# A fused gated recurrence and MLP: the first product in seven block products over two of its three feature tiles, and no latency inside an engine in the plan

## The chip, the cores and the metric

The kernel runs on one core of a Trainium2 chip. The core has a matrix engine (TensorE, PE in the profile; its weight loads are PEld), a vector engine (DVE), an activation engine (ACT), GpSimd (POOL) and a queue engine (SP), each of which works through its own instruction list in order. They wait for each other through semaphores. The metric is the device time in microseconds (us) of a whole execution. A second record of the same kernel is the profile of one execution, whose span goes from its first to its last instruction.

## The reference, cut to what matters

A gated linear recurrence over 768 positions for 4 x 8 heads of 48 features gives 3072 tokens of 384 features. They go through a two-layer block with the activation h - tanh(h).

```python
for t in range(S):                      # per batch and head
    state = alpha[t][:, None] * state + k[t][:, None] * v[t][None, :]
    y[t] = q[t] @ state
x = y.transpose(0, 2, 1, 3).reshape(3072, 384)
h = x @ w_in                            # 384 -> 2048
g = h - tanh(h)
return g @ w_out                        # 2048 -> 384
```

All is float32. The kernel takes h - tanh(h) as a polynomial in h, and checks on the chip that the arguments are small enough for it.

## The kernel before, in words

**Tiles and loops.** The 3072 tokens are cut into 12 units (NU) of 256 tokens (TU), that is two token tiles of 128. For each unit `gla(u)` does the recurrence in a chunked form and leaves the unit's tokens transposed in `xT[u]`: 128 features by 256 tokens in each of three feature tiles (KT = 3). A fourth feature tile is working space; `moves` copies 16-row pieces from it into the first three by DMA. Then `moe(u)` goes over 8 steps (FS), each with two tiles of 128 of the 2048 hidden features. There are two buffers of `xT`.

**One step.** `first` (line 1078) computes h for two hidden tiles a and the unit's 256 tokens: for each a three products, one per feature tile j, of a 128 x 128 weight block and 256 token columns (line 1083). h fills one of two PSUM banks (`ps_h`). On ACT, `square` (line 1092) makes u from h squared and `quad` (line 1096) makes z from u. On DVE, `cube` (line 1100) multiplies h and u into w, and `shrunk` (line 1104) makes g from z and w. After two steps `large` (line 1110, ACT) looks for arguments that are too big. For units from the third on (`PLAIN` = 2) the second product is itself a block product with seven terms: `sums` (lines 1116 to 1118, DVE) makes five combinations e of blocks of g, and `second` (line 1149) does seven products of 192 columns onto four PSUM accumulators o, with weight combinations b that `combine 0` to `combine 4` have made from w_out once. Units 0 and 1 use line 1128 instead. After eight steps `store` takes the accumulators out.

**Buffers.** u, z and w have two buffers (u holds two steps in each), g and e have three. A bank of h is free when `cube` has read it.

**The order.** It isn't the program's order of loops. A `Planner` gets every piece of work as a task with an engine, a duration in us, a rank and the names of the tasks that it waits for. It simulates the engines: the start of a task is after the ends of those it waits for, plus a latency (0.3 us unless the task says otherwise, whatever the two engines are). It does eight rounds of list scheduling with priorities from the latest starts, keeps the round that ends earliest, and issues the instructions in that order. Two tasks that follow in a chain of the same kind without a named dependence have latency 0 on the same engine. On the chip semaphores alone decide when an instruction runs; the plan fixes only each engine's order. Idle PE time at the beginning is filled with products of an identity matrix (line 1211).

**Work beside the steps.** The recurrence of a later unit (on DVE: 32 x 32 transposes at line 641, scans at 713 and 732, scalings at 737, and smaller sums; on ACT: copies at 635, 918 and 999), and `look`, which reloads weights and checks their size on ACT (lines 104 and 105).

Of the kernel before, what the change touches and what calls it, by code (L numbers as in the profile page):

```python
# [9 lines left out]
FP32 = mybir.dt.float32  # L10
# [7 lines left out]
P = 128  # L18
HP = 64
CU = 2  # L20
# [301 lines left out]
class Planner:  # L322
# [13 lines left out]
    def add(self, name, engine, us, rank, after, do, lat=0.3):  # L336
        kind = name.rsplit(" ", 1)[0]
        self.tasks.append((name, engine, us, rank, [a for a in after if a], do, lat, self.last.get(kind)))
        self.last[kind] = name
# [47 lines left out]
    def order(self):  # L387
        names = {t[0]: i for i, t in enumerate(self.tasks)}
        assert len(names) == len(self.tasks)
        before, after = ([[] for _ in self.tasks] for _ in range(2))  # L390
        for i, t in enumerate(self.tasks):
            edges = {names[a]: self.tasks[names[a]][6] for a in t[4]}
            if t[7]:
                edges.setdefault(names[t[7]], 0.0 if self.tasks[names[t[7]]][1] == t[1] else 0.25)
            for j, lat in edges.items():
                before[i].append((j, lat))
                after[j].append((i, lat))
# [17 lines left out]
        for x in plan:  # L415
            name, e, length = self.tasks[x[3]][:3]
            if e == engine and until:
# [3 lines left out]
                free = x[0] + length  # L421
# [5 lines left out]
def fast(tc, q, k, v, alpha, moe_w_in, moe_w_out, out, w_in, w_out, ident, ok, pad_rows):  # L427
# [11 lines left out]
    NH = d_model // 2  # L439
    PLAIN = 2  # L440
    V, A, T, GP = nc.vector, nc.scalar, nc.tensor, nc.gpsimd

    out_r = out.rearrange("(t p) n -> t p n", p=P)

    with ExitStack() as ctx:
# [159 lines left out]
        def gla(u, rank):  # L605
# [166 lines left out]
            def chunk(c):  # L772
# [7 lines left out]
                def go_c(name, engine, us, k, after, do, **kw):  # L780
                    add(f"{name} {me}", engine, us, rank + 6 * c + k,
                        [a if a[-1] in "0123456789" else f"{a} {me}" for a in after if a], do, **kw)
# [200 lines left out]
                if not last:  # L983
                    go_c("state", "DVE", 0.26, 10, ["mid", n > 0 and not past_last and f"y {past}"], state)
                go_c("y", "PE", 1.29, 9, ["masked", "mid", not last and "state", n > 0 and "decay",
                                         u == 1 and c and f"x {past}", u == 1 and c and f"rest {past}"], halves_products)
                go_c("x", "ACT", 0.5, 10, ["y"], features)
                go_c("rest", "DVE", 0.87 if u >= PLAIN else 1.02, 10.5, ["x"], rest)

# [60 lines left out]


        looked = {}

# [13 lines left out]
        def moe(u, rank, gait):  # L1067
            m = {}
            plain = u < PLAIN

            def step(s):
# [15 lines left out]

                def square():
                    if s % 2 == 0:
                        m["us", s // 2] = two.tile([P, 2, 2 * TU], FP32, name="u")  # L1090
                    m["u", s] = m["us", s // 2][:, s % 2]
                    A.activation(m["u", s], m["h", s], AF.Square, scale=W_SCALE ** -1.5)  # L1092

# [4 lines left out]
                def cube():  # L1098
                    m["w", s] = two.tile([P, 2 * TU], FP32, name="w")
                    V.tensor_mul(m["w", s], m["h", s], m["u", s])  # L1100
# [18 lines left out]

                def second():  # L1120
                    g = m["g", s]
                    if plain:
# [7 lines left out]
                        return  # L1130
                    if s == 0:
                        m["o"] = [ps_o.tile([P, 2, NH], FP32, name=f"o{n}") for n in range(2 * CU)]
# [10 lines left out]
                    if u == NU - 1 and s == FS - 2:  # L1143
                        now, m["rest"] = now[:4], now[4:]
                    elif u == NU - 1 and s == FS - 1:
                        now = now[:4] + m["rest"][:2] + now[4:6] + m["rest"][2:] + now[6:]

                    for s_, n, i, g_, w_ in now:
                        T.matmul(o[n][:, i], lhsT=g_, rhs=w_, start=(s_ == 0 and (n, i) in ((0, 0), (1, 0), (2, 1), (3, 0))),  # L1149
                                 stop=(s_ == FS - 1), skip_group_check=True)  # L1150

                add(f"first {me}", "PE", 2.59, r,
                    [f"in{s}" if plain else None, f"cube {older[2]}" if older[2] else f"masked 0.{CU - 1}"]
                    + [f"x {u}.{c}" if u == 0 else f"moves {u}" for c in range(CU if u == 0 else 1)], first)

                add(f"square {me}", "ACT", 0.5, r + 0.9,
                    [f"first {me}"] + ([f"large {older[3]}", f"cube {older[3]}", f"quad {older[3]}"]
                                       if s % 2 == 0 and older[3] else []), square)
                add(f"cube {me}", "DVE", 0.6, r + 0.9, [f"square {me}", older[2] and f"shrunk {older[2]}"], cube)
# [5 lines left out]
                if not plain:  # L1165
                    add(f"sums {me}", "DVE", 0.85, r + 1.1, [f"shrunk {me}"], sums)
                add(f"second {me}", "PE", 2.58 if plain else 1.3 if me == f"{NU - 1}:{FS - 2}" else 3.28 if me == f"{NU - 1}:{FS - 1}" else 2.28, r + 5,
                    [f"out{s}" if plain else "combine 4", f"sums {me}" if not plain else f"shrunk {me}"]
                    + ([f"store {n}" for n in range(max(0, u - 2 if u <= PLAIN else u - 1), u)] if s == 0 and u >= PLAIN else [])
                    + ([f"state {PLAIN - 1}.{c}" for c in range(CU) if (PLAIN - 1) % UPB * CU + c < NCH - 1]  # L1170
                       + [f"rest {PLAIN - 1}.{CU - 1}"] if u == PLAIN - 1 and s == 0 else [])
                    + ([f"second {u}:{s - 1}"] if s else []), second)

# [151 lines left out]
```

## Time and profile before

| | us |
|---|---|
| median of three runs | 576.95 (576.02 to 577.92) |
| the profiled execution, span | 574.2 |
| PE busy | 564.0 |
| DVE busy | 450.9 |
| ACT busy | 323.2 |
| one step's first product (line 1083, 12 records), in the chain | 2.59 |
| one unit in the steady stretch | 44.80 |

The profiled execution has only its span, from first to last instruction; no total of that execution is recorded. The 2.75 us between the span and the median of the runs are what lies around the instructions, and the difference between executions. Busy time is the union of an engine's intervals. Ends of matrix instructions are modelled, so the start of the next one is the better mark. A float32 product appears as two records. A group's line gives the source line, engine, operation, output and inputs with shapes, the count, busy time and mean duration in ns, and the idle time ahead of it with what ended it.

### The profile page before, as it was taken

How to read it: one execution, taken by the hardware profiler on the slowest of the kernel's cores; microseconds unless marked ns; L12 is line 12 of the kernel's file. 1: busy time of each engine (PE TensorE's matmuls, PEld its weight loads, DVE VectorE, ACT ScalarE, POOL GpSimd, SP SyncE). 2: the span in 40 equal slices, each digit the busy share in tenths (PEclk: the TensorE clock that was granted, in tenths of full speed). 3: DMA queues.
4: the chain of work that ended last, by engine and by line, in shares of the span. 5: the costliest groups of instructions: out<-in, count | busy, mean ns of one | idle time of the engine just before them, and what ended most of it. 6: DMA issues, size and time to landing. Idle time of an engine off the chain costs nothing.

```text
span 574.2 us, 13772 instructions
## 1 busy us (share of the span) xinstructions
PE 564.0 (98%) x5595; PEld 498.0 (87%) x5595; DVE 450.9 (79%) x886; ACT 323.2 (56%) x559; POOL 4.8 (1%) x22
## 2 busy tenths in 40 slices
PE   8999999999999999999999999999999999999995
PEld 8877677778999989998998999899898999899995
DVE  6988879999999996896895895896797745544643
ACT  3689996747687675676584374364353433333530
POOL 3000000000000000000000000000000000000000
PEclk9999999999999999999999999999999999999999
DMA  8889792336674852562630320310200000000001
GB/s 179 200 223 252 254 169 63 93 77 137 114 143 122 171 116 93 117 144 85 169 114 7 82 60 2 84 50 14 58 8 1 30 7 3 29 8 0 29 2 34
DMA packets 60713, 50.84 MB, mean 89 GB/s; under 512 B 35776, under 2 KB 50400, under 8 KB 60640
## 3 DMA queue, kind: packets, MB, share of 16 engines
q1 hardware_dynamic: 57728, 48.88, 34.8%
q10 hardware_dynamic: 2912, 0.98, 0.8%
q8 instruction: 46, 0.75, 0.6%
q14 instruction: 27, 0.22, 0.1%
HBM read 44.04 MB, written 4.72 MB: 85 GB/s over the span
## 4 chain that ended last, share of the span: by engine, by line
PE 95%; DMA 2%; SPq 1%; ACT 1%; DVE 0%; issue 0%; POOL 0%; DVEq 0%; ACTq 0%; POOLq 0%
PE h L1083 42%; PE o L1149 33%; PE o L1128 7%; PE sc L808 2%; PE sc L881 2%; PE sc L814 2%; PE sc L891 2%; DMA raw<-in_moe_w_in_dram 2%; PE sc L994 1%; PE spin L1211 1%; SPq L43 1%; PE turned L665 1%; PE scores L798 0%; SPq L597 0%; PE sc L665 0%
## 5 line engine op out<-in xcount | busy, mean ns | idle before, releaser
L1083 PE MATMUL h<-xT,w_in 128*128 128x256 f32 x1152 | 265.5, 380 | 1.2 <-DVE w_in L90 1.1
L1083 PEld LDWEIGHTS h<-xT,w_in 128*128 128x128 f32 x1152 | 215.2, 190 | 29.4 <-DVE w_in L90 2.7
L1092 ACT ACTIVATE u<-h 128x512 f32<-128x512 f32 x96 | 56.9, 592 | 175.3 <-PE h L1083 174.8
L1100 DVE TENSOR_TENSOR w<-h,u 128x512 f32<-128x512 f32 x96 | 66.0, 689 | 79.0 <-ACT u L1092 78.7
L1149 PE MATMUL o<-b,e 128*128 128x192 f32 x480 | 90.9, 326 | 0.0
L1149 PE MATMUL o<-w_out,e 128*128 128x192 f32 x320 | 81.4, 337 | 0.0
L1149 PEld LDWEIGHTS o<-b,e 128*128 128x128 f32 x480 | 80.2, 190 | 0.0
L1104 DVE SCALAR_TENSOR_TENSOR g<-z,w 128x512 f32<-128x512 f32 x96 | 65.7, 685 | 3.1 <-ACT z L1096 0.2
L1149 PE MATMUL o<-b,g 128*128 128x192 f32 x320 | 65.1, 326 | 0.0
L1096 ACT ACTIVATE z<-u 128x512 f32<-128x512 f32 x96 | 60.4, 629 | 2.6
L1149 PEld LDWEIGHTS o<-w_out,e 128*128 128x128 f32 x320 | 55.7, 190 | 4.4
L1149 PEld LDWEIGHTS o<-b,g 128*128 128x128 f32 x320 | 54.2, 190 | 0.0
L1110 ACT ACTIVATE big<-u 128x1024 f32<-128x1024 f32 x48 | 50.4, 1050 | 0.0
L1128 PE MATMUL o<-w_out,g 128*128 128x384 f32 x128 | 44.0, 488 | 0.0
L1128 PEld LDWEIGHTS o<-w_out,g 128*128 128x128 f32 x128 | 24.1, 190 | 13.7
L1116 DVE TENSOR_TENSOR e<-g 128x256 f32<-128x256 f32 x80 | 33.6, 420 | 1.8
L1117 DVE TENSOR_TENSOR e<-g 128x256 f32<-128x256 f32 x80 | 33.5, 419 | 0.0
L641 DVE STREAM_TRANSPOSE aT<-ar 128x256 f32<-128x256 f32 x44 | 28.4, 646 | 2.8 <-ACT ar L635 1.7
L732 DVE TENSOR_TENSOR_SCAN W<-aT,before 128x1032 f32<-128x1032 f32 (+1 forms) x13 | 27.8, 2135 | 0.0
L713 DVE TENSOR_TENSOR_SCAN U<-aT,after 128x1032 f32<-128x1032 f32 (+1 forms) x13 | 27.6, 2128 | 0.1
L1118 DVE TENSOR_TENSOR e<-g 128x128 f32<-128x128 f32 x80 | 22.9, 287 | 0.0
L86 ACT ACTIVATE more<-raw 128x768 int16<-128x768 uint32 x16 | 17.2, 1074 | 7.1 <-DMA raw<-in_moe_w_out_dram 2.8
(138 smaller groups left out, 559.9 us busy)
## 6 DMA issues: line engine op xcount, KB each, us to landing
raw<-in_moe_w_out_dram SPq DMA_DIRECT2D x16, 768.0 KB, 5.2
raw<-in_moe_w_in_dram SPq DMA_DIRECT2D x80, 96.0 KB, 4.4
raw<-in_moe_w_in_dram SPq DMA_DIRECT2D x16, 288.0 KB, 4.7
vt<-in_v_dram SPq DMA_DIRECT2D x23, 192.0 KB, 4.4
ar<-in_alpha_dram SPq DMA_DIRECT2D x44, 96.0 KB, 2.7
kr<-in_k_dram SPq DMA_DIRECT2D x40, 96.0 KB, 2.3
qr<-in_q_dram SPq DMA_DIRECT2D x40, 96.0 KB, 2.3
out_dram<-cross SPq DMA_DIRECT2D x19, 96.0 KB, 1.7
```

What stands on the lines that cost most here:

```text
L641: V.transpose(to, raws[what][:, g, :, 0:32])
L732: V.tensor_tensor_scan(out=m["W"][:, ns].rearrange("p n t -> p (n t)"), data0=aT[:, a:z], data1=before[:, a:z], initial=0.0, op0=ALU.mult, ...
L1083: T.matmul(h[:, a, :], lhsT=w_in[:, j, f * P:(f + 1) * P], rhs=xT[u][:, j, :], start=(j == 0), stop=(j == KT - 1))
L1092: A.activation(m["u", s], m["h", s], AF.Square, scale=W_SCALE ** -1.5)
L1096: A.activation(m["z", s], m["u", s], AF.Square, bias=QB, scale=QA * W_SCALE)
L1100: V.tensor_mul(m["w", s], m["h", s], m["u", s])
L1104: V.scalar_tensor_tensor(out=g.rearrange("p a c t -> p (a c t)"), in0=m["z", s], scalar=QK, in1=m["w", s], op0=ALU.add, op1=ALU.mult)
L1110: A.activation(big, m["us", s // 2].rearrange("p s t -> p (s t)"), AF.Relu, bias=-U_FAST, scale=W_SCALE, accum_out=over[:, n:n + 1])
L1116: V.tensor_add(e[:, 0:2, :], g[:, 0], g[:, 1])
L1117: V.tensor_sub(e[:, 2:4, :], g[:, :, 1, :], g[:, :, 0, :])
L1128: T.matmul(m["o"][c], lhsT=g[:, a, c, :], rhs=w_out[:, f, :], start=(f == 0), stop=(f == FT - 1))
L1149: T.matmul(o[n][:, i], lhsT=g_, rhs=w_, start=(s_ == 0 and (n, i) in ((0, 0), (1, 0), (2, 1), (3, 0))), stop=(s_ == FS - 1), skip_group_ch ...
```

## The change

**The first product.** For units from the fourth on (`SEVEN` = 3), two feature tiles and two hidden tiles against two token tiles form a 2 x 2 block product, which is done with seven products of 128 columns instead of eight (as four of 256 columns). The third feature tile is done as before, two products of 256 columns. The seven need combinations of weight blocks and of token blocks:

- `weigh 0` to `weigh 4` (DVE, once) make four combinations of w_in over all steps, three of them in a part of w_out that is no longer read, one in place of a block of w_in.
- `mix u` (DVE, per unit) makes four combinations of token blocks, in the fourth feature tile of `xT`, in a new tile, and in place of one block.

A step's product becomes a chain: two products, a copy on ACT of both results into u; a third product added onto one of them, a copy; a fourth added onto the same, a copy; three more, each onto one quarter; the third feature tile onto all four quarters. `join` on DVE adds the bank and the kept copies into w, and `square` and `cube` read w instead of the bank. The bank is free after `join`. `second` is issued in four tasks of 2, 2, 1 and 2 products, except in the last two steps.

**The plan.** The latency between two tasks of one engine, SP left out, is 0 instead of 0.3 us. The task `x` gets a named dependence on the last first product of two units before.

```diff
-            edges = {names[a]: self.tasks[names[a]][6] for a in t[4]}
+            edges = {names[a]: 0.0 if self.tasks[names[a]][1] == t[1] != "SP" else self.tasks[names[a]][6] for a in t[4]}
...
+    SEVEN = 3
...
-                go_c("x", "ACT", 0.5, 10, ["y"], features)
+                go_c("x", "ACT", 0.5, 10, ["y", u > 1 and f"first {u - 2}:{FS - 1}"], features)
...
+        wi = w_in.rearrange("p k (s a n) -> p k s a n", a=2, n=P)
+        free = w_out.rearrange("p (s a) n -> p s (a n)", a=2)[:, :, NH:3 * NH].rearrange("p s (i n) -> p s i n", n=P)
+        left = {1: wi[:, 0, :, 0], 2: wi[:, 1, :, 0], 3: free[:, :, 2], 4: wi[:, 1, :, 1], 5: free[:, :, 0], 6: free[:, :, 1], 7: wi[:, 0, :, 1]}
+        def weigh(n):
+            if n == 0:
+                V.tensor_add(left[5], wi[:, 0, :, 1], left[4])
+            elif n == 1:
+                V.tensor_sub(left[6], left[5], left[1])
+            elif n == 2:
+                V.tensor_sub(left[3], left[2], left[6])
+            else:
+                at = slice((n - 3) * FS // 2, (n - 2) * FS // 2)
+                V.tensor_sub(left[7][:, at], left[1][:, at], left[7][:, at])
+        for n in range(5):
+            add(f"weigh {n}", "DVE", 1.2 if n < 3 else 0.7, 2 * FS * (SEVEN - 1) + (n if n < 3 else 8 * (n - 2)),
+                ["combine 4", f"second {PLAIN - 1}:{FS - 1}"] + [n > 2 and f"first {SEVEN - 1}:{(n - 2) * FS // 2 - 1}"], lambda n=n: weigh(n))
+        def mix(u):
+            x, more = xT[u], combo_pool[0].tile([P, P], FP32, name="more_x", bufs=2)
+            (b11, b12), (b21, b22) = ([x[:, k, h * P:(h + 1) * P] for h in range(2)] for k in range(2))
+            t1, t2 = (x[:, KT, h * P:(h + 1) * P] for h in range(2))
+            right[u] = {1: b11, 2: b21, 3: b22, 4: more, 5: t1, 6: t2, 7: b12}
+            V.tensor_sub(t1, b12, b11)
+            V.tensor_sub(t2, b22, t1)
+            V.tensor_sub(more, b21, t2)
+            V.tensor_sub(b12, b22, b12)
...
+                def product(n, to, start=False):
+                    T.matmul(m["h", s][:, to], lhsT=left[n][:, s], rhs=right[u][n], start=start, stop=True, skip_group_check=True)
+                def seven_a():
+                    m["h", s] = ps_h.tile([P, 4, P], FP32, name="h")
+                    product(1, 3, True)
+                    product(5, 1)
+                def keep(n):
+                    if n == 0:
+                        take_u()
+                        m["kept", s] = m["u", s].rearrange("p (i t) -> p i t", t=P)
+                        A.copy(m["kept", s][:, 0::3], m["h", s][:, 3::-2])
+                    else:
+                        A.copy(m["kept", s][:, n], m["h", s][:, 3])
+                def seven_d():
+                    for n, to in ((2, 0), (3, 1), (4, 2)):
+                        product(n, to)
+                def seven_e():
+                    for a in range(2):
+                        T.matmul(m["h", s][:, 2 * a:2 * a + 2].rearrange("p i t -> p (i t)"), lhsT=wi[:, KT - 1, s, a], rhs=xT[u][:, KT - 1, :],
+                                 start=False, stop=True, skip_group_check=True)
+                def join():
+                    m["w", s] = two.tile([P, 2 * TU], FP32, name="w")
+                    V.tensor_add(m["w", s], m["h", s].rearrange("p i t -> p (i t)"), m["u", s])
+                    m["h", s] = m["w", s]
...
+                if seven:
+                    add(f"first_a {me}", "PE", 0.45, r, [bank, f"mix {u}", "weigh 0"], seven_a)
+                    add(f"keep_a {me}", "ACT", 0.38, r + 0.1, [f"first_a {me}"] + old_u, lambda: keep(0))
+                    add(f"first_b {me}", "PE", 0.224, r + 0.2, [f"keep_a {me}", "weigh 1"], lambda: product(6, 3))
+                    add(f"keep_b {me}", "ACT", 0.26, r + 0.3, [f"first_b {me}"], lambda: keep(1))
+                    add(f"first_c {me}", "PE", 0.224, r + 0.4, [f"keep_b {me}", f"weigh {3 + 2 * s // FS}"], lambda: product(7, 3))
+                    add(f"keep_c {me}", "ACT", 0.26, r + 0.5, [f"first_c {me}"], lambda: keep(2))
+                    add(f"first_d {me}", "PE", 0.67, r + 0.6, [f"keep_c {me}", "weigh 2"], seven_d)
+                    add(f"first {me}", "PE", 0.86, r + 0.65, [f"first_d {me}"], seven_e)
+                    add(f"join {me}", "DVE", 0.65, r + 0.7, [f"first {me}", older[2] and f"shrunk {older[2]}"], join)
...
+                parts = [7] if not seven or (u == NU - 1 and s >= FS - 2) else [2, 4, 5, 7]
```

## The prediction

> **What bounds the kernel now.** I read the page first (busy times, the 40 slices, the chain that ended last, the costliest groups), then stretches of one unit each, then single groups.
>
> ```profile
> PE 564.0 (98%) x5595; PEld 498.0 (87%) x5595; DVE 450.9 (79%) x886; ACT 323.2 (56%) x559; POOL 4.8 (1%) x22
> PE   8999999999999999999999999999999999999995
> DVE  6988879999999996896895895896797745544643
> ACT  3689996747687675676584374364353433333530
> PE 95%; DMA 2%; SPq 1%; ACT 1%; DVE 0%; issue 0%; POOL 0%; DVEq 0%; ACTq 0%; POOLq 0%
> L1083 PE MATMUL h<-xT,w_in 128*128 128x256 f32 x1152 | 265.5, 380 | 1.2 <-DVE w_in L90 1.1
> L1149 PE MATMUL o<-b,e 128*128 128x192 f32 x480 | 90.9, 326 | 0.0
> ```
>
> 95% of the chain is PE, and the two groups show almost no idle time before them: TensorE is the bound, and nothing it waits for matters. Each float32 product has two records (1152 for 576 products). The next view gives busy time by engine for the opening units of the changed stretch, two middle ones and the last full ones.
>
> ```profile
> core 0: us, PE busy (x) PEld busy (x) DVE busy (x) ACT busy (x) POOL busy (x), PEclk, DMA share, GB/s
> 137.00:167.50 30.50, 30.50 (x320) 28.19 (x310) 30.24 (x63) 21.90 (x42) 0.00 (x0) 1.00 0.63 121
> 167.50:212.30 44.80, 44.80 (x474) 40.94 (x474) 43.68 (x86) 33.41 (x62) 0.00 (x0) 1.00 0.67 144
> 257.10:301.90 44.80, 44.80 (x472) 40.94 (x473) 37.06 (x76) 31.23 (x58) 0.00 (x0) 1.00 0.43 122
> 346.70:391.50 44.80, 44.80 (x458) 40.94 (x457) 36.47 (x74) 20.95 (x37) 0.00 (x0) 1.00 0.18 48
> 436.30:481.10 44.80, 44.80 (x474) 40.94 (x473) 25.61 (x61) 16.23 (x28) 0.00 (x0) 1.00 0.04 13
> 481.10:525.90 44.80, 44.80 (x396) 41.06 (x395) 23.79 (x54) 15.33 (x27) 0.00 (x0) 1.00 0.04 12
> ```
>
> Unit 3, the first to change, starts its first products at 167.5, and every unit takes 44.80 us, all PE. DVE has 7 to 8 us to spare per unit in the middle, 1 us in unit 3, and 19 us and more at the end.
>
> The chain in order of time gives the price of a step:
>
> ```profile
> 251.12 2.61 PE h L1083 x12
> 330.24 2.59 PE h L1083 x12
> 558.42 4.55 PE o L1149 x28
> ```
>
> A first product is 2.59 us, 0.4325 per product of 256 columns; a second one 2.28 (7 x 0.326). 8 x 4.87 = 38.96 of the 44.80 are these; 5.84 is the recurrence of the unit ahead.
>
> **What the skill says.** The Trainium skill, TensorE: Matmul & The Clock Gate, LDWEIGHTS: a load takes its columns over 1.2, so 107 ns for 128. A 128-column product has two loads beside two passes, so loads could bound it. The trace has such a product, the idle filler:
>
> ```profile
> 10.54 1.38 PE L1211 MATMUL spin<-ident 128*128 128x128 f32 x10
> L923 ACT COPY xT<-y 128x256 f32<-128x256 f32 x1 | 0.4, 372 | 0.6 <-PE y L863 0.6
> L923 ACT COPY xT<-y 128x128 f32<-128x128 f32 x1 | 0.3, 272 | 0.0
> L1100 DVE TENSOR_TENSOR w<-h,u 128x512 f32<-128x512 f32 x96 | 66.0, 689 | 79.0 <-ACT u L1092 78.7
> ```
>
> The first gap is 0.213 (cold start) and the last record lasts 0.275, so the eight gaps between are (1.38 - 0.213 - 0.275) / 8 = 0.112 us, and a product of two costs 0.2235, load and pass in step; the page's price agrees. The same page, table at the head: ACT and DVE are strict first-in first-out, PE can only pull loads ahead. That decides how a late wait spreads. ScalarE: Activation LUTs, What ACT_TABLE_LOAD costs: 186 ns + 0.833 ns an element; 293 for 128, the trace has 272. VectorE: DVE Perf Modes, the perf-mode tier table: float32 tensor_tensor has one rate, SBUF or PSUM; the trace agrees (689 with a PSUM input, 685 at line 1104 without).
>
> **Removed and added on PE.** Per step, six products of 256 (2.595) become seven of 128 (7 x 0.2235 = 1.5645) and two of 256 (0.865): 2.4295. The saving is 0.1655; 9 units x 8 steps = 72 steps give **11.9 us**, the most the change can bring. The second product is cut into parts of 2, 2, 1 and 2 products, with no further instruction: free, as PE changes between the two kinds now at no visible gap.
>
> **The chain it adds.** Products 1 and 5, a copy on ACT, product 6 onto the same columns, a copy, product 7, a copy, three products, then the third tile. Each copy must end before PE goes on. In the timeline line 1083's last pass starts at 404.91 and takes 0.216, and ACT starts at 405.33, 0.20 us after it; from a copy's end to PE's start it shows 0.05 (38.19 to 38.24, line 1002 to line 814). So the three loops are 0.20+0.37+0.05 = 0.62, and twice 0.20+0.27+0.05 = 0.52: 1.66 us a step. Bare, that is 120 us over 72 steps. The cover: four parts of a second product (2.28), the other h bank's chain, and 5.84 / 8 = 0.73 of recurrence per step. That is more than enough if it is ready. The plan prices the loops 0.98 and twice 0.86, so each has some 0.35 of slack against the trace. Two banks: a bank comes back after about 5 us of chain plus join, and two steps last 10.6, so the banks do not bind.
>
> Queued behind a late wait on PE is everything, second products and the recurrence's too; behind a copy on ACT, the squares and so the cubes. The trace of before shows no PE wait of this sort in the steady stretch, so I bound it: 0 if the plan's slack holds; and above, one keep in five late by 0.3 us, 216 x 0.2 x 0.3 = 13 us, all of the gain. I take one in ten by 0.2, that is 4.3 us: the slack speaks for few, ACT's long pieces (1.05 + 0.19 for line 1110, 1.8 for a look) for some.
>
> **ACT** gains 0.372 + 2 x 0.272 = 0.92 a step, 7.3 a unit. With 33.4 that is 40.7 of 43.5 in unit 3; with 20.95 it is 28. The square reads SBUF instead of PSUM: 629 against 592, 0.3 a unit.
>
> **DVE** gains the join, 0.69 (5.5 a unit), and mix, four dependent 128-column operations, some 0.29 each: 1.15. With 36.5 that is 43.1 against a new PE unit of 44.80 - 1.32 = 43.48; in unit 3, with 43.68, it is 50.3, besides weigh (three at 1.22 as at line 737, two at 0.69: 5 us, partly before 167.5). That is over. What hides it is work ahead: in the timeline the recurrence of unit 4 (line 903) ends on DVE at 192.6, for products that start at 212.3, 20 us early. Units 3 to 8 can spend that, then the recurrence ends and DVE is at 75%. So DVE's sum does not bind, but its queue is full, so joins and sums come late at times. I put this at 0.2 to the same 4.3 us, no further term; none and 8 us as its ends.
>
> **The plan without in-engine latency.** It adds no instruction and only reorders, in units 0 to 2 too. The engines run as soon as they can, and dependent DVE operations cost 0.72 from start to start (line 1104 at 405.24, line 1116 at 405.96) where the plan now says 0.60. In units 0 to 2 PE is full either way: I take 0, and 1.5 us either way. The wait of x on the older first product and the later one for weigh 3 and 4 come after work 20 us old: 0.
>
> **The end.** The last step gets a join: 0.69 + 0.04 before its square. Now 4.55 us of second products cover that stretch (the last line above) and the last e parts come just in time, so I count 0.8; between 0 and 2.
>
> **Sum.** 574.2 - 11.9 + 4.3 + 0.8 = 567.4 of span. The profiled execution's own total is not given; the median of 576.95 lies 2.75 above the span, which I carry: **570.2**.
>
> **Rivals.**
> A, as above: loops mostly covered. 60%, 565 to 575; most likely 570.2.
> B, gain given back: waits of 0.15 a step, 72 x 0.15 = 10.8 and the end 0.8, total 576.7. For it: ACT at 94% and DVE full in unit 3. Against: later units have room. 10%.
> C, slower: DVE's queue binds in units 3 to 8. Joins stand behind the recurrence's 2.30 us scans and 1.22 us products; a join frees an h bank and leads to the sums, so PE finds neither a chain nor a second part ready. If DVE's 43.1 a unit grows by 3.4 of dependency gaps to 46.5, six units lose 1.7 each (+10.2), three gain 1.32 (-4.0), the end adds 0.8: 584. It decides from 1.32 us of PE idle a unit. For it: 99% of a period. Against: 20 us of lead and PE's full rate in 137 to 212 with DVE at 98%. 28%.
> D, the products don't shrink, because single ones behind a wait expose their 0.11 us load: 72 x 3 x 0.11 = 24 us if always; only with PE empty, so it comes with C. 2%.
>
> **Numbers.** A difference under 0.3% (1.7 us) is about what a measurement can't tell from none. A lies beyond it nearly whole; B is split. Faster 0.62, same 0.08, slower 0.30. Range: below, the full saving with nothing given back and a little from the order, 565; above, C up to its price, 584. A's own range is 565 to 575.
>
> **What would show it.** Seven-product steps of 2.43 us on PE; line 1083's group gone from units 3 to 11; unit periods of 43.5 to 44.2, shortest in units 9 to 11; PE idle attributed to ACT copies of some 4 us in all. Wrong if PE idles over 12 us there, if it waits for DVE's sums or joins, or if units 9 to 11, with DVE at 75%, do not shorten.

## The result, and the profile after

The changed kernel takes 593.36 us (593.26 to 593.72). The ratio to the kernel before is 1.0283, with a 95% interval of 1.0260 to 1.0306: slower, where 570.2 had been forecast. The profiled execution took 593.31 us, its span is 591.6.

The page of the changed kernel, the lines that answer to those of before:

```profile
PE 561.5 (95%) x6021; PEld 506.6 (86%) x6021; DVE 518.3 (88%) x999; ACT 375.9 (64%) x775; POOL 4.8 (1%) x22
...
PE   8969999999989999999989999999999999999995
...
DVE  7599889999999998999999899899999976775754
...
DVE 49%; PE 34%; ACT 7%; issue 6%; DMA 2%; SPq 1%; DVEq 0%; POOL 0%; ACTq 0%; POOLq 0%
...
L1128 PE MATMUL h<-xT,w_in 128*128 128x128 f32 x432 | 87.1, 287 | 10.2 <-ACT u L1141 4.9
...
L1154 DVE TENSOR_TENSOR w<-h,u 128x512 f32<-128x512 f32 x72 | 49.3, 685 | 16.7 <-PE h L1149 16.2
```

The chain that ended last was 95% TensorE; it is now 49% DVE and 34% PE. DVE is at 88% of the whole span, and its slices stand at 8 and 9 from the third to the thirty-second: over three quarters of the run it hardly rests. The new products (line 1128) wait 10.2 us before them in one of their groups, and the join (line 1154) adds 49.3 us of DVE's time.

The next view is the busy time by engine in units 4 to 7 and in units 9 and 10 of the changed kernel:

```profile
core 0: us, PE busy (x) PEld busy (x) DVE busy (x) ACT busy (x) POOL busy (x), PEclk, DMA share, GB/s
229.10:279.90 50.80, 47.77 (x542) 44.71 (x540) 48.25 (x92) 37.86 (x85) 0.00 (x0) 1.00 0.40 99
279.90:326.60 46.70, 43.96 (x517) 41.17 (x516) 45.09 (x89) 33.33 (x75) 0.00 (x0) 1.00 0.44 111
326.60:372.20 45.60, 43.38 (x496) 40.52 (x494) 42.97 (x86) 31.99 (x71) 0.00 (x0) 1.00 0.23 64
372.20:418.10 45.90, 45.25 (x532) 42.92 (x528) 42.95 (x85) 28.16 (x64) 0.00 (x0) 1.00 0.16 43
...
463.90:506.90 43.00, 43.00 (x465) 41.47 (x464) 31.63 (x70) 21.74 (x53) 0.00 (x0) 1.00 0.04 13
506.90:545.90 39.00, 38.52 (x356) 36.85 (x355) 28.29 (x61) 20.75 (x51) 0.00 (x0) 1.00 0.04 14
```

Before, such a stretch was 44.80 us with PE busy in all of it and DVE with 36 or 37. Now the four units are longer, units 4 and 5 the most: PE stands still for about 3 us in each of these two, and DVE is busy for 95% of the first and 97% of the second. In units 9 and 10 the recurrence has ended, DVE has room, and the units are shorter than before.

A unit is marked here and below by its first write of z on ACT. In the kernel before that comes 3 to 6 us after the first products that the prediction counted from; in the changed kernel the first product of unit 3 starts at 170.6, 14 us ahead of the mark. Some of a unit's PE work falls on either side of the mark, so stretches of several units are surer than one:

| stretch, us | before | after |
|---|---|---|
| start to unit 3 | 173.0 | 184.9 |
| unit 3 | 43.7 | 44.2 |
| units 4 to 8 | 223.1 | 234.8 |
| of that, DVE busy | 182.7 | 222.7 |
| units 9 to 11 | 134.5 | 127.7 |
| span | 574.2 | 591.6 |

By these marks the changed kernel is 11.9 us behind at unit 3, falls back 12.3 more in units 3 to 8, and wins 6.8 at the end.

What PE waits for in units 3 to 8 of the changed kernel (us in total, times, longest):

```profile
PE h L1128 <- ACT u L1141: 4.9, 10, 0.8
PE h L1128 <- DVE w L1154: 4.3, 9, 1.4
PE h L1128 <- ACT u L1139: 1.2, 2, 0.7
PE o L1219 <- DVE e L1185: 0.9, 2, 0.6
```

In the kernel before this view has no row in the same units. Copies on ACT and joins on DVE share the waits about equally; which of them rules can't be read from here, since a copy that comes late can be late because its bank was.

The saving itself is there. If every PE record of the first and second products in units 4 to 10 is given its undisturbed spacing (0.112, 0.163 and 0.216 us for 128, 192 and 256 columns), the sum is 273.4 us before and 263.2 after, 10.2 less. What the records take beyond that rises from 4.6 to 20.0.

The same account over the whole run depends little on where a mark falls. The 384-column products of units 0 and 1 are priced at 0.324 us and the recurrence's records at their mean spacing in the kernel before; it is an estimate, worked out from the two traces. The priced work falls by 11.6 us. What PE takes beyond the price, by waiting, at half clock or in uneven spacing, grows by 8.1 us up to the mark of unit 3, by 19.2 in units 3 to 8 and by 1.7 after them. I call this growth over the kernel before PE's loss. The other 3.8 of the 11.9 us at unit 3 are work that PE did ahead of the mark and not time lost.

In the opening the two timelines of PE part early. The changed kernel:

```profile
37.54 0.98 PE L995 MATMUL y<-ident,kT 112*128 112x112 f32 x8 [1.65 <-DVE kT L682]
41.68 1.13 PE L809 MATMUL sc<-qT,kT 48*64 48x64 f32 x32 [3.15 <-DVE qT L682]
...
43.78 3.67 PE L1117 MATMUL h<-xT,w_in 128*128 128x256 f32 x12 [0.15 <-DVE w_in L90]
```

The kernel before:

```profile
38.24 0.68 PE L814 MATMUL sc<-vt,kn 64*64 64x48 f32 x32 [0.77 <-ACT kn L1002]
38.86 2.86 PE L1083 MATMUL h<-xT,w_in 128*128 128x256 f32 x12
```

The new plan brings the next unit's recurrence forward on PE, and PE then stands 1.65 and 3.15 us for scalings on DVE that aren't done. The same twelve records of a first product take 3.67 us there instead of 2.86: the granted clock is at half for 6.8 us from 38.6 on. Shortly before the mark of unit 3 PE stands another 2.3 us for the recurrence's state on DVE (line 953).

### The profile page after: what moved, and what is told of

Same layout as the page of the kernel before. It is cut to its first block, busy times and chain, and to the rows that moved or that the text cites. A ratio compares the mean times of both kernels' runs of the same rounds, so it can differ in the third digit from the quotient of the medians.

```text
span 591.6 us, 14961 instructions
## 1 busy us (share of the span) xinstructions
PE 561.5 (95%) x6021; PEld 506.6 (86%) x6021; DVE 518.3 (88%) x999; ACT 375.9 (64%) x775; POOL 4.8 (1%) x22
## 4 chain that ended last, share of the span: by engine, by line
DVE 49%; PE 34%; ACT 7%; issue 6%; DMA 2%; SPq 1%; DVEq 0%; POOL 0%; ACTq 0%; POOLq 0%
PE o L1219 12%; PE h L1128 8%; DVE g L1173 6%; DVE w L1169 5%; DVE aT L642 5%; PE h L1149 4%; DVE w L1154 4%; DVE U L714 3%; DVE kT L642 3%; DVE W L733 3%; PE h L1117 3%; DVE e L1186 3%; DVE qT L642 2%; DVE e L1185 2%; DVE xT L904 2%
## 5 line engine op out<-in xcount | busy, mean ns | idle before, releaser
L1128 PE MATMUL h<-xT,w_in 128*128 128x128 f32 x432 | 87.1, 287 | 10.2 <-ACT u L1141 4.9
L1160 ACT ACTIVATE u<-w 128x512 f32<-128x512 f32 x72 | 45.4, 630 | 66.9 <-DVE w L1154 66.7
L1128 PEld LDWEIGHTS h<-xT,w_in 128*128 128x128 f32 x432 | 69.7, 190 | 19.1 <-ACT u L1141 8.3
L1128 PE MATMUL h<-xT,w_out 128*128 128x128 f32 x432 | 84.1, 276 | 1.2 <-ACT u L1139 1.2
L1149 PE MATMUL h<-xT,w_in 128*128 128x256 f32 x288 | 74.1, 380 | 0.0
L1128 PEld LDWEIGHTS h<-xT,w_out 128*128 128x128 f32 x432 | 68.5, 191 | 3.1 <-ACT u L1139 1.9
L1141 ACT COPY u<-h 128x128 f32<-128x128 f32 x144 | 37.1, 260 | 53.5 <-PE h L1128 52.8
L1219 PE MATMUL o<-b,g 128*128 128x192 f32 x320 | 70.9, 326 | 0.0
L1117 PE MATMUL h<-xT,w_in 128*128 128x256 f32 x288 | 67.9, 386 | 1.8 <-DVE rough L475 1.1
L1117 PEld LDWEIGHTS h<-xT,w_in 128*128 128x128 f32 x288 | 54.2, 192 | 11.7 <-DVE rough L475 1.5
L1154 DVE TENSOR_TENSOR w<-h,u 128x512 f32<-128x512 f32 x72 | 49.3, 685 | 16.7 <-PE h L1149 16.2
L1169 DVE TENSOR_TENSOR w<-w,u 128x512 f32<-128x512 f32 x72 | 49.0, 681 | 10.1 <-ACT u L1160 9.8
L1149 PEld LDWEIGHTS h<-xT,w_in 128*128 128x128 f32 x288 | 49.2, 191 | 3.7
```

Source lines behind the costliest of these rows:

```text
L1117: T.matmul(h[:, a, :], lhsT=w_in[:, j, f * P:(f + 1) * P], rhs=xT[u][:, j, :], start=(j == 0), stop=(j == KT - 1))
L1128: T.matmul(m["h", s][:, to], lhsT=left[n][:, s], rhs=right[u][n], start=start, stop=True, skip_group_check=True)
L1149: T.matmul(m["h", s][:, 2 * a:2 * a + 2].rearrange("p i t -> p (i t)"), lhsT=wi[:, KT - 1, s, a], rhs=xT[u][:, KT - 1, :], start=False, st ...
L1154: V.tensor_add(m["w", s], m["h", s].rearrange("p i t -> p (i t)"), m["u", s])
```

## The experiments

All totals are medians; the ratio is to the kernel before on the same chip (its medians there are 575.4 to 576.5), with its 95% interval. "DVE" is DVE's busy time on the page, "unit 3" its start, "4 to 8" the length of these units, with DVE's busy time in them in brackets, both by the marks. lat_dve, lat_rest and pad_join have two executions each.

| run | total, us | ratio | DVE | unit 3 | 4 to 8 (DVE) |
|---|---|---|---|---|---|
| before | 576.49 | | 450.9 | 173.0 | 223.1 (182.7) |
| after | 593.36 | 1.0283 [1.0260, 1.0306] | 518.3 | 184.9 | 234.8 (222.7) |
| lat_only | 584.27 | 1.0141 [1.0087, 1.0196] | 463.0 | 179.3 | 224.0 (189.8) |
| seven_only | 578.10 | 1.0046 [1.0028, 1.0063] | 506.0 | 172.5 | 222.7 (207.7) |
| short_join | 577.94 | 1.0049 [1.0029, 1.0069] | 487.0 | 186.5 | 222.9 (204.7) |
| no_loop | see below | | | 187.0 | 236.1 (222.8) |
| pad_join | 606.59 | 1.0525 [1.0493, 1.0557] | 535.0 | 186.5 | 243.0 (232.1) |
| lat_dve | 586.19 | 1.0178 [1.0148, 1.0207] | 462.4 | 180.7 | 224.0 (189.1) |
| lat_rest | 581.87 | 1.0103 [1.0065, 1.0140] | 451.3 | 174.6 | 223.9 (183.6) |
| lat_013 | 575.82 | 0.9994 [0.9984, 1.0004] | 455.5 | 172.9 | 224.0 (186.3) |
| seven_dve | 597.19 | 1.0373 [1.0349, 1.0397] | 517.6 | 185.9 | 229.1 (216.9) |
| seven_rest | 581.56 | 1.0089 [1.0048, 1.0130] | 507.1 | 184.9 | 224.4 (208.7) |
| seven_gp | 576.66 | 1.0017 [1.0001, 1.0032] | 482.2 | 173.2 | 226.3 (202.0) |
| gp2_3 | 577.26 | 1.0038 [1.0019, 1.0056] | 498.2 | 174.9 | 222.2 (207.5) |
| gp2_8 | 579.31 | 1.0053 [1.0030, 1.0075] | 477.4 | 176.2 | 225.5 (190.7) |
| seven9_old | 574.06 | 0.9985 [0.9971, 0.9999] | 473.7 | 171.5 | 220.7 (185.8) |

### The two halves of the change, each alone

lat_only is the kernel before with the latency edit:

```diff
-            edges = {names[a]: self.tasks[names[a]][6] for a in t[4]}
+            edges = {names[a]: 0.0 if self.tasks[names[a]][1] == t[1] != "SP" else self.tasks[names[a]][6] for a in t[4]}
```

> The kernel before with the latency edit alone; no seven-product step. Theory O (the edit itself spoils the order of units 0 to 2, so that the fourth unit starts at 185 instead of 173 us): 586 to 590, the fourth unit at 183 to 187, DVE and PE order of units 0 to 2 as in the changed kernel. Theory W (the 12 us of the opening come from the new tasks, weigh and mix, on a full DVE, or from the plan being chosen for its end): within 2 us of 576.5, the fourth unit at 172 to 175.

seven_only is the changed kernel with that line put back:

> The whole change but for the latency edit: dependent tasks of one engine keep 0.3 us in the plan. Theory O: the opening is whole again (fourth unit at 173 to 177) and the total falls by some 10 us to 581 to 585, slower than before by what DVE costs in units 3 to 8. Theory W: the fourth unit still starts at 181 or later and the total stays at 590 or above.

The latency edit alone costs 1.41%, somewhat less than I had expected of it, and unit 3 starts 6.3 us late. PE's order from 26 to 56 us is the changed kernel's, with the same two waits; this is the timeline of lat_only:

```profile
41.68 1.13 PE L808 MATMUL sc<-qT,kT 48*64 48x64 f32 x32 [3.15 <-DVE qT L681]
...
43.77 3.67 PE L1083 MATMUL h<-xT,w_in 128*128 128x256 f32 x12 [0.15 <-DVE w_in L90]
```

So the opening's loss begins with the latency edit. The seven products alone cost 0.46%, less than expected too, but they gain nothing. Together the parts come to 1.87% and the whole change to 2.83%: some 5.5 us appear only when both are there. PE's loss shows where. lat_only loses 8.3 us before unit 3 and nothing in units 3 to 8; seven_only loses nothing before unit 3, 10.7 in units 3 to 8 and 3.6 after; the changed kernel 8.1, 19.2 and 1.7. What only the two together bring lies in units 3 to 8.

### What limits units 3 to 8

short_join is the changed kernel with the join done on 64 of 512 columns, which takes load off DVE and leaves PE's and ACT's work as it is:

```diff
-                    V.tensor_add(m["w", s], m["h", s].rearrange("p i t -> p (i t)"), m["u", s])
-                    m["h", s] = m["w", s]
+                    V.tensor_add(m["w", s][:, 0:64], m["h", s].rearrange("p i t -> p (i t)")[:, 0:64], m["u", s][:, 0:64])
+                    m["h", s] = m["u", s]
```

> The changed kernel with its join done for 64 of 512 columns; square and cube then work on u, so the activation is taken of something else. Every task, its order and every wait stays; DVE does some 0.5 us less in each of 72 steps (36 us). Theory D (DVE is the bound in units 4 to 8, rival C of the prediction): units 4 to 8 fall from 45.6 to 50.8 us each to 43.5 to 44.5, the total from 593.4 to 578 to 583. Theory L (PE waits for the copies on ACT in its chain): those units change by less than 0.5 us each, total above 589.

no_loop is the changed kernel in which the copies don't wait for PE:

```diff
-                        A.copy(m["kept", s][:, 0::3], m["h", s][:, 3::-2])
+                        A.copy(m["kept", s][:, 0::3], xT[u][:, 0, :].rearrange("p (i t) -> p i t", t=P))
...
-                        A.copy(m["kept", s][:, n], m["h", s][:, 3])
+                        A.copy(m["kept", s][:, n], xT[u][:, 0, 0:P])
```

> The changed kernel with its three copies per step reading xT in SBUF instead of the bank, so that PE never waits for a copy within the chain; what is joined is then something else. ACT and DVE do the same amount of work. Theory D: units 4 to 8 stay at 45 to 50 us each, total 589 to 594. Theory L: they fall to 43.5 to 44.5, total 578 to 583.

In no_loop the kernel's general path ran as well, after the part studied here, so its total (2699.75 us) says nothing and only its units are read. Without the round trips through ACT, units 4 to 8 take 236.1 us, as long as with them, and PE's loss in units 3 to 8 is 18.9 us (19.2 with them). The waits have moved to the joins and sums:

```profile
PE h L1128 <- DVE w L1154: 8.7, 12, 2.4
PE o L1219 <- DVE e L1185: 2.3, 3, 0.9
```

With DVE's load cut, units 4 to 8 take 222.9 us, 44.6 each and unit 4 still 47.6, somewhat more than theory D had; the total of 577.94 is just under its range. From the mark of unit 3 to the end short_join needs 392.4 us, 8.8 less than the kernel before, of which some 2 are work done ahead of the mark. While DVE is as full as in the changed kernel, the copies that PE was seen to wait for set nothing.

short_join lightens DVE and shortens the join at once. pad_join keeps the short join and puts load back elsewhere, as two additions of 224 columns behind the sums, which nothing reads (0.39 us each):

```diff
+                    if seven:
+                        pad = two.tile([P, 224], mybir.dt.bfloat16, name="pad", bufs=1)
+                        for x in range(2):
+                            V.tensor_add(pad, g.rearrange("p a c t -> p (a c t)")[:, 224 * x:224 * x + 224], g.rearrange("p a c t -> p (a c t)")[:, 224:448])
```

> The kernel with the short join (64 of 512 columns, activation of something else), and two further additions of 224 columns after each step's sums, whose results nobody reads: DVE is as full as in the changed kernel, but the chain from the last product to the square and to the free bank keeps the short join. If it is DVE's sum of work that counts: back to 590 to 595, units 4 to 8 at 45.5 us and more each. If it is the length of the join in the chain: 577 to 581 as with the short join alone.

Busy time by engine in units 4 and 6, first in short_join:

```profile
229.50:277.10 47.60, 46.39 (x534) 43.48 (x532) 43.81 (x91) 38.06 (x85) 0.00 (x0) 1.00 0.40 101
...
320.80:365.40 44.60, 43.53 (x503) 41.60 (x503) 40.42 (x87) 32.21 (x70) 0.00 (x0) 1.00 0.24 65
```

Then in pad_join:

```profile
233.70:285.80 52.10, 48.45 (x538) 44.09 (x536) 50.00 (x108) 37.86 (x84) 0.00 (x0) 1.00 0.39 98
...
334.90:382.10 47.20, 43.60 (x496) 40.51 (x495) 44.62 (x102) 32.02 (x70) 0.00 (x0) 1.00 0.23 62
```

The total of 606.59 us lies above both ranges: the two additions put 0.78 us a step on DVE where the short join had taken off 0.47, so DVE is fuller than in the changed kernel, not as full. PE's busy time in unit 6 is the same (43.53 and 43.60); the unit is 2.60 longer where DVE has 4.20 more. pad_join's joins are as short as short_join's, and still PE waits for them: the view of its waits has these rows over units 3 to 8, where short_join has none for a join.

```profile
PE h L1128 <- DVE w L1154: 8.8, 13, 1.9
PE h L1128 <- ACT u L1141: 8.2, 13, 1.4
```

It is DVE's amount of work, then, not the join's length. Over units 3 to 8 together the kernels give a curve (seven_rest and seven_dve are described below):

| units 3 to 8 | DVE busy, us | share of their length | PE's loss, us |
|---|---|---|---|
| before | 223.5 | 84% | 0 |
| lat_only | 232.1 | 86% | 0.0 |
| short_join | 245.4 | 92% | 4.7 |
| seven_rest | 250.3 | 94% | 10.0 |
| seven_only | 255.0 | 94% | 10.7 |
| seven_dve | 259.2 | 94% | 17.6 |
| after | 265.4 | 95% | 19.2 |
| pad_join | 277.2 | 96% | 28.8 |

The change was to save 6 x 1.32 = 7.9 us here, and with 250 us of DVE's time the loss is already larger. The share tells the rows apart badly, because PE's waits lengthen the units too. Where between 232 and 245 us the loss begins is open. So is what the chain of copies costs when DVE has room: in short_join PE waits 2.0 us for copies and not for joins, and no run takes the copies away there.

### Why the latency edit costs

On the kernel before I set the latency to zero for one set of engines at a time, and then for all of them to 0.13 (the three lines stand for lat_dve, lat_rest and lat_013 in turn):

```diff
-            edges = {names[a]: self.tasks[names[a]][6] for a in t[4]}
+            edges = {names[a]: 0.0 if self.tasks[names[a]][1] == t[1] == "DVE" else self.tasks[names[a]][6] for a in t[4]}
...
+            edges = {names[a]: 0.0 if self.tasks[names[a]][1] == t[1] and t[1] not in ("SP", "DVE") else self.tasks[names[a]][6] for a in t[4]}
...
+            edges = {names[a]: 0.13 if self.tasks[names[a]][1] == t[1] != "SP" else self.tasks[names[a]][6] for a in t[4]}
```

> The kernel before with latency 0 between tasks of DVE alone. If it is DVE's chains, priced below what they cost (0.72 us from start to start where the plan then says 0.60), that spoil the opening: 582 to 585, the fourth unit 6 to 9 us late. If it is ACT's or PE's: 575 to 578.

> The kernel before with latency 0 between tasks of ACT and of PE, not of DVE. If DVE's chains spoil the opening: 575 to 578. If ACT's or PE's: 582 to 585. If both: each takes a part of the 9 us.

> The kernel before with 0.13 us between dependent tasks of one engine, about what the trace shows on top of the planned durations, instead of 0.3. If the opening suffers because a latency of 0 is below the true cost: 575 to 578. If any departure from 0.3 sends the planner to another, worse order: 580 to 586.

Either half does harm, and the two don't add up (1.78% and 1.03% against 1.41% for both), as may be when each gives another order. The totals, 586.19 and 581.87, lie just above and just below the 582 to 585 written down. Nearly all of it is lost in the opening: PE's loss before unit 3 is 9.7 us in lat_dve and 4.2 in lat_rest, and neither loses more than 0.1 us in units 3 to 8. At 0.13 us, about what a dependent pair was seen to cost over an independent one, the loss is gone. Zero is a wrong price here. That 0.13 helps because it is the true cost, and not because it happens to give a good order, rests on this one value.

The page shows where the price is paid. With the same 886 instructions, DVE is busy 450.9 us before and 463.0 in lat_only; with the same 999, 506.0 in seven_only and 518.3 in the changed kernel. Hardly any operation became longer (the durations add up to 572.9 and 575.0 us in the last two). They follow each other in another order. The timeline of DVE in the changed kernel:

```profile
386.19 0.68 DVE L1169 TENSOR_TENSOR w<-w,u 128x512 f32<-128x512 f32 x1
386.97 0.69 DVE L1173 SCALAR_TENSOR_TENSOR g<-z,w 128x512 f32<-128x512 f32 x1
387.70 0.43 DVE L1185 TENSOR_TENSOR e<-g 128x256 f32<-128x256 f32 x1
```

In seven_only:

```profile
338.19 0.68 DVE L1173 SCALAR_TENSOR_TENSOR g<-z,w 128x512 f32<-128x512 f32 x1
338.79 0.68 DVE L1169 TENSOR_TENSOR w<-w,u 128x512 f32<-128x512 f32 x1
339.39 0.42 DVE L1185 TENSOR_TENSOR e<-g 128x256 f32<-128x256 f32 x1
```

Each line is a start, a duration and an operation. In the first the shrink (g) reads the w made just before it and starts 0.78 after it, and the sum reads that g and starts 0.73 after it. In the second another step's cube lies between, no operation reads its neighbour's output, and starts are 0.60 apart: the next one begins 0.08 before the last one's record ends. In the seven-product steps, cube and shrink follow directly on each other 17 times in seven_only and 63 times in the changed kernel, shrink and sum 19 and 73 times. From start to start that is 46 x 0.19 + 54 x 0.13 = 15.8 us. It isn't the same thing as the 12.3 us more on the page, which counts an overlap once and a gap not at all. The overlaps of all neighbours on DVE add up to 67.5 us in seven_only and 57.1 in the changed kernel, and with the 2.1 us of longer records that is about the 12.3. The gaps inside the pairs named, 2.8 us in seven_only and 11.0 in the changed kernel, come on top as idle time of a full engine. The Trainium skill, VectorE: DVE Perf Modes, The DRAIN you can't avoid, says of a chain of copies that the semaphore after each costs nothing extra; for these operations the measurement differs, by 0.13 to 0.19 us a pair.

That was a reading of traces that were already there, so I tested it in the changed kernel, with the zero for DVE alone and for ACT and PE alone (seven_dve and seven_rest in turn):

```diff
-            edges = {names[a]: 0.0 if self.tasks[names[a]][1] == t[1] != "SP" else self.tasks[names[a]][6] for a in t[4]}
+            edges = {names[a]: 0.0 if self.tasks[names[a]][1] == t[1] == "DVE" else self.tasks[names[a]][6] for a in t[4]}
...
+            edges = {names[a]: 0.0 if self.tasks[names[a]][1] == t[1] and t[1] not in ("SP", "DVE") else self.tasks[names[a]][6] for a in t[4]}
```

> The whole change, with the latency zero between tasks of DVE alone (0.3 us on ACT and PE). Theory Q (with zero on DVE the plan puts a cube, its shrink and its sums directly behind one another; each dependent pair costs 0.73 to 0.80 us from start to start where a pair with other work between costs 0.60, and that is some 12 us of DVE's time over the run): DVE's busy time on the page 515 to 520 us, units 4 to 8 together 231 to 238 us, total 589 to 597. Theory O (the zero latency costs only through the order of the opening, and DVE's time is the same either way): DVE 504 to 508, units 4 to 8 together 221 to 226, total 580 to 587.

> The whole change, with the latency zero between tasks of ACT and of PE alone (0.3 us on DVE). Theory Q: DVE keeps its other work between dependent operations, DVE's busy time 504 to 508 us, units 4 to 8 together 221 to 226 us as in seven_only, and only the opening's order costs, as in lat_rest: total 580 to 587. Theory O: the same totals here; theory P (PE's and ACT's zero does the harm in the middle): units 4 to 8 together 231 to 238 us, total 589 to 597.

DVE's busy time came out at 517.6 and 507.1 us and the totals at 597.19 and 581.56, the first just over the edge of what theory Q gave, the second inside. Units 4 to 8 of seven_rest take 224.4 us, those of seven_dve 229.1, somewhat less than the 231 to 238 written down. Theories O and P are out for DVE's time and for the middle. They keep a part in the opening: seven_rest reaches unit 3 as late as the changed kernel (184.9) with DVE's time unchanged, so there the order on PE and ACT is enough to lose it (PE's loss before unit 3 is 7.1 us, against 8.1). What each task of the opening adds was not taken apart.

### Ways out

seven_gp is seven_only with `mix`, `weigh` and two of the three sums on GpSimd:

```diff
-                V.tensor_add(left[5], wi[:, 0, :, 1], left[4])
+                GP.tensor_add(left[5], wi[:, 0, :, 1], left[4])
...
-                    V.tensor_sub(e[:, 2:4, :], g[:, :, 1, :], g[:, :, 0, :])
-                    V.tensor_add(e[:, 4, :], g[:, 0, 0, :], g[:, 1, 1, :])
+                    if not seven:
+                        more_sums(V)
...
+                        add(f"sums_g {me}", "POOL", 1.2, r + 1.1, [f"sums {me}"], lambda: more_sums(GP))
```

> The seven-product kernel with the plan's latencies left at 0.3 us, and DVE relieved: mix, weigh and two of the three sums of a step run on GpSimd, some 0.5 us a step and 1.2 us a unit less for DVE. Theory D (DVE's sum is what eats the saving in units 3 to 8): those units fall to 43.5 to 44.3 us each, the total to 564 to 570, faster than before. Theory L (the chain through ACT): no more than 2 us off the 578.1 of the kernel without relief.

It came to 576.66, 1.4 below seven_only: not theory D's 564 to 570, but inside the range written for theory L. That doesn't make the copies the cause, since in its units 3 to 8 PE waits 3.7 us for joins and 0.2 for a copy. DVE is 23.8 us lighter on the page, and units 4 to 8 are no shorter. In units 3 to 8 DVE is busy for 246.0 us, as in short_join, and PE's loss is 8.8 us where short_join has 4.7: DVE's time alone doesn't set it. Three groups of the page:

```profile
L1191 POOL TENSOR_TENSOR e<-g 128x256 f32<-128x256 f32 x72 | 75.6, 1050 | 244.3 <-DVE g L1173 177.7
...
L1169 DVE TENSOR_TENSOR w<-w,u 128x512 f32<-128x512 f32 x72 | 54.7, 759 | 10.1 <-ACT u L1160 9.7
L1192 POOL TENSOR_TENSOR e<-g 128x128 f32<-128x128 f32 x72 | 55.0, 764 | 0.0
```

The two sums take 1.05 + 0.76 = 1.81 us one behind the other, where the plan had 1.2, and the cube on DVE 759 ns where it takes 683 in seven_only. gp2_3 (shown against seven_gp) therefore leaves only the last sum on GpSimd and lets only the last part of a second product wait for it; gp2_8 does the same with seven products from unit 8 on.

```diff
-                    E.tensor_sub(e[:, 2:4, :], g[:, :, 1, :], g[:, :, 0, :])
...
-                    r + 5 + 0.1 * n, needs if n == 1 else [f"second_{n - 2} {me}"],
+                    r + 5 + 0.1 * n, needs if n == 1 else [f"second_{n - 2} {me}", f"sums_g {me}"],
...
-    SEVEN = 3
+    SEVEN = 8
```

> Seven products from the fourth unit on, latencies at 0.3; on GpSimd now mix, weigh and only the last, smallest sum, which just the last part of a second product waits for. DVE gives off 0.2 us a step and 1.2 a unit. If the earlier relief failed because GpSimd's sums came late (1.8 us for two where the plan had 1.2): 570 to 575. If relief of DVE does not help: 576 to 579.

> The same from the ninth unit on: four units, three of them with DVE at 55% or less. 571 to 573.5, 0.4 to 0.8% faster than before, if those units save 1.0 us each as their two block forms would have it; 574 or more if the saving there is only what SEVEN = 9 gave.

Neither gained. gp2_3, at 577.26, fell into the range written for a relief that does not help. It did help where it was aimed, in units 3 to 8, where PE's loss is 7.1 us against seven_only's 10.7, and lost 3.1 more than seven_only before unit 3. gp2_8, at 579.31, lies in the open-ended "574 or more" and is slower than the kernel before. It starts unit 3 3.2 later and unit 8 8.1 later, before any step that was changed, and wins 3.1 back after that. An edit of the task list reorders what lies ahead of it too. How much of GpSimd's failure is its lateness, the slower DVE operations beside it, or the plan's order, these runs don't separate.

seven9_old takes seven products only where the recurrence has ended, in units 9 to 11, with the old latency:

```diff
-    SEVEN = 3
+    SEVEN = 9
```

> Seven products in the last three units alone (SEVEN = 9), latencies at 0.3 us: there DVE is at 55% before. Theory D: the three units each save 1.0 to 1.3 us, total 572 to 573.5 against 576.0 before, or 0.4 to 0.7% faster. Theory L: the chain costs as much there as in the middle, total 576 to 578.

574.06 us, 0.15% below the kernel before, where 572 to 573.5 had been expected. The interval just leaves out 1, for one of fifteen versions, so this is hardly a gain; it is the only version of the seven products that isn't slower. Three units could give 24 x 0.1655 = 4.0 us at most.

## Why the prediction was wrong

**Removed and added on PE, 11.9 us.** Right in size: the priced work on PE fell by 11.6 us over the run. The rival in which the products don't shrink is out, as the 128-column records keep a median spacing of 0.112 us in units 3 to 8 as well.

**The chain it adds, 4.3 us.** Such waits exist, 6.1 us in all for both sorts of copy over units 3 to 8, but no_loop removes what they wait for and the units stay as long. So the term was near what is listed, and what is listed was not what cost the time. Whether the cover that I named would do with more room on DVE isn't shown.

**DVE, "no further term".** This step failed. Its sum of 43.1 us a unit was nearly right (215.5 for five units, against 207.7 in seven_only and 222.7 after), but I set 43.1 against PE's 43.48 and let a lead of 20 us pay for what comes late. A lead is a stock, and an engine at 99% can't refill it; the lengths of units 3 and 4 (44.2 and 50.8 us) fit a lead that is soon used up, but no run tests it. seven_only shows the size without the other edit: PE's loss is 10.7 us in units 3 to 8 and 3.6 after, where I had 4.3 for this and the copies together. In the changed kernel it is 19.2 in units 3 to 8, and short_join, with 31.3 us less of DVE's time, takes the stretch from unit 3 to the end from 406.7 to 392.4 us, 14.3 less. Both are beyond the 8 that I had set as the upper end. One price beside it holds: the join with an input in PSUM takes 685 ns, the cube with both in SBUF 681. Rival C had the place and the mechanism; its 3.4 us a unit were called dependency gaps, and such gaps are what the next step brings.

**The plan without in-engine latency, "0, and 1.5 us either way".** This failed as well, and it is the larger part of the error: 1.41% alone, about 8 us, and in the changed kernel 15.3 (578.10 without it, 593.36 with it). "It adds no instruction and only reorders" was true, and the conclusion was wrong twice. The two starts 0.72 apart that I quoted, beside 0.60 in the plan, were the price of a dependent neighbour; I didn't ask how many more such neighbours the plan would make if it believed them free. That is 12 us of DVE's busy time, which the kernel before can hide from unit 3 on (224.0 us for units 4 to 8 in lat_only, with PE busy in all of them) and the changed kernel can't. And in units 0 to 2, "PE is full either way" does not hold: PE waits 1.65 and 3.15 us, its clock halves for 6.8, and PE's loss before unit 3 is 8.1 us.

**The end, 0.8.** Not separable. PE's loss from unit 9 on is 1.7 us as a whole, of which the last join is a part. Units 9 to 11 are 6.8 us shorter by the marks, more than their own 4.0, because work of theirs was done earlier.

The errors add up. The forecast's span was 567.4 and 591.6 was measured, 24.2 more. PE's loss was 8.1 + 19.2 + 1.7 = 29.0 us where 4.3 + 0.8 = 5.1 had been forecast, 23.9 more, and the saving was 0.3 smaller. Of the signs I had named, units 9 to 11 did shorten, and the sign against, waits for joins, appeared. Rival C's 584 is 9.4 too low, and most of that is the opening, which it left out.

## What to carry to other kernels

When work moves to another engine, compare its new busy share with what the runs show and not with 100%: here PE lost nothing over six units with DVE at 86%, 4.7 us at 92%, and more than the whole saving of 7.9 at 94%. A planner's latency inside an engine is a price, not a margin: at zero it sets dependent operations side by side, and an engine near its limit pays each pair, with no instruction added. A wait listed for the bound engine names the last to arrive, and it can stand behind another engine's queue, so test it by lightening the suspected engine and by loading it again elsewhere, before believing the name.

## What was not expected of the hardware

- Behind a float32 operation of 512 columns on DVE the next one starts after 0.60 us when it doesn't read that one's output, and after 0.73 to 0.80 when it does.
- In the changed kernel PE's clock was at half for 6.8 us from 38.6 on, after a gap of 1.65 us (35.9 to 37.5) and as one of 3.15 began (38.5). That is twice the idle window of about 3.4 us after which, by the Trainium skill, TensorE: Matmul & The Clock Gate, Part 1, the clock falls to half. No gap here was that long, so in this trace a whole idle window was not needed. seven_only had one such spell, of 3.4 us, at 229.0, behind gaps of 1.21 and 1.61, and the kernel before had none before its end.
- A float32 addition of two SBUF inputs on GpSimd took 1.05 us for 256 columns and 0.48 to 0.76 for 128. In the same run (seven_gp) the cube on DVE, 512 columns with two SBUF inputs, went from 683 to 759 ns, while the join, with one input in PSUM, stayed at 683.
